# Spreading attention's pieces over all fourteen products of a chunk

## The chip, the cores and the metric

The kernel runs on one core of a Trainium2 chip. The time is device microseconds of one execution, and the median of several executions counts. The core has TensorE (matmul; PE in the profile, its weight loads PEld), VectorE (DVE), ScalarE (ACT), GpSimd (POOL) and SyncE (SP), which here issues transfers between HBM and the on-chip memory SBUF. Matmul results land in PSUM, which the other engines empty. The program gives each engine its own list of instructions; where one needs what another engine or a transfer has yet to make, it waits.

## What is computed

Attention with a decay (retention) over 8 batches, 8 heads, 576 positions and head width 64, and then a two-layer block over the 8 x 576 = 4608 tokens:

```python
scores = scale * np.matmul(q, k.transpose(0, 1, 3, 2))
gamma = 1.0 - 2.0 ** (-5.0 - np.arange(H, dtype=np.float32))
Dmat = np.where(rel >= 0, gamma[:, None, None] ** rel[None, :, :], 0.0)
ret = scores * Dmat[None, :, :, :]
attn_out = np.matmul(ret, v)
# x: (B,H,S,D) -> (B*S, H*D) = 4608 x 512
h = x @ w_in                       # 512 x 2048
sp = np.maximum(h, 0.0) + np.log1p(np.exp(-np.abs(h)))
g = h * erf(sp)
return (g @ w_out).astype(np.float32)   # 2048 x 512
```

## The kernel before

Tokens are handled in 9 chunks of 512. The hidden width is cut in 4 groups, so there are 36 pairs of a first layer and a second layer (`First(g, c)`, `Second`); the first nine pairs are group 0 of each chunk. Each layer of a pair is done in seven products in place of eight (a Strassen-like scheme), a product being four matmuls of 128 x 128 by 128 x 256 in fp32, which the profile shows as eight. So a chunk of one group has fourteen products.

Attention makes the chunks' x while group 0 runs. It goes in 36 pieces of 128 positions, four to a chunk, numbered from 0. A piece has three stages: `transposes` (q and k turned, here by VectorE out of tiles that were loaded as squares), `scores` (32 matmul records, masked by VectorE) and `outputs` (values, state and the x of the piece). The stages stand in one list, and the loop over products takes from it.

The stages (the transposes for pieces from 12 on are VectorE's; the branch with TensorE is cut). The load of q and k of piece i + 2 is issued behind the transposes of piece i; their tiles have two buffers:

```python
    def transposes(i):
        t = live[i] = loaded.pop(i)
        if i < SQUARES:
            weigh_values(i)
        for name in "qk":
            tT = t[name + "T"] = att.tile([P, NP, P], FP32, tag=name + "T", name=name + "T")
            if name + "s" in t:
                for _, _, n, r0 in pieces[i]:
                    a = r0 // SQ * D
                    squares = t[name + "s"][:, :, a : a + n // SQ * D].rearrange("p h (a d) -> p h a d", d=D)
                    order = "p h (a r) -> p h a r" if name == "q" else "p h (r a) -> p h a r"
                    nc.vector.transpose(
                        out=tT[:, :, r0 : r0 + n].rearrange(order, r=SQ), in_=squares[:, :, :, :SQ]
                    )
            else:
                # [... transposes by TensorE for the first pieces ...]
        load(i + 2, "q")

    def scores(i):
        # [... matmuls into ps[0], ps[1] ...]
        mask = tri if len(pieces[i]) == 1 else tri2
        for e in range(2):
            tt(sT[:, e], ps[e], mask.unsqueeze(1).to_broadcast([P, NP, P]), ALU.mult)

    def outputs(i):
        # [... matmuls: values, state update (kv), state times q ...]
        # [... VectorE: sums and state; then x of the piece: ...]
        scaled(1)
        scaled(0)
        load(i + 3, "kv")
        if i + 1 >= SQUARES:
            weigh_values(i + 1)

    stages = [(transposes, 0), (scores, 0)]
    for i in range(len(pieces)):
        stages += [(transposes, i + 1), (outputs, i), (scores, i + 1)]
        if i in (PC + 1, 2 * PC - 1):
            stages[-3:-1] = stages[-2], stages[-3]
    stages = [(of, i) for of, i in stages if i < len(pieces)]
    done = [0]

    def before_chunk(c):

        return stages.index((outputs, c * PC)) if c < n_ch else len(stages)

    def after_chunk(c):

        return stages.index((outputs, (c + 1) * PC - 1)) + 1

    held = [False]

    def attend_next(upto):

        if done[0] < upto and stages[done[0]][0] is outputs:
            held[0] = not held[0]
            if held[0]:
                return
            attend(done[0] + 1)
        attend(min(done[0] + 1, upto))

    def attend(upto):
        while done[0] < min(upto, len(stages)):
            of, i = stages[done[0]]
            of(i)
            done[0] += 1

    PLAIN = 2
```

The products of the first layer (those of the second have the same form). `yield` ends a product; the accumulators `a`, `e` and `g` lie in PSUM, `e` and `g` with one buffer each:

```python
        def first(self):
            self.a = ps_a.tile([P, W], FP32, tag="a", name="a1")
            e = ps_e.tile([P, W], FP32, tag="e", name="e1")

            self.t1 = gpool.tile([P, 2, W], FP32, tag="t1", name="t1")
            self.product(A11, self.a, True)
            nc.scalar.copy(out=self.t1[:, 0], in_=self.a)
            yield
            self.product(A12, e, True)
            tt(self.t1[:, 0], e, self.t1[:, 0], ALU.add)
            yield

        def middle(self):
            self.e = ps_e.tile([P, W], FP32, tag="g", name="g1")
            self.t2 = gpool.tile([P, 2, W], FP32, tag="t2", name="t2")
            self.product(S2, self.a, False)
            nc.scalar.copy(out=self.t1[:, 1], in_=self.a)
            yield
            self.product(S3, self.e, True)
            yield
            self.product(S1, self.a, False)
            nc.scalar.copy(out=self.t2[:, 1], in_=self.a)
            tt(self.t2[:, 1], self.e, self.t2[:, 1], ALU.add)
            yield

        def last(self):
            self.product(S4, self.a, False)
            nc.scalar.copy(out=self.t2[:, 0], in_=self.a)
            yield
            self.product(A22, self.e, False)
            tt(self.t1[:, 1], self.e, self.t1[:, 1], ALU.add)
            self.softplus()
            yield
```

The second layer's products around the accumulator g (`take` empties into the output tile, by ScalarE in group 0; `add` by VectorE):

```python
        def first(self):
            self.a = ps_a.tile([P, 2, OH], FP32, tag="a", name="a2")
            e = ps_e.tile([P, 2, OH], FP32, tag="e", name="e2")
            self.product(B11, self.a, True)
            self.take(0, 0, self.a)
            yield
            self.product(B21, e, True)
            self.add(0, 0, e)
            yield

        def middle(self):
            self.e = ps_e.tile([P, 2, OH], FP32, tag="g", name="g2")
            self.product(T2, self.a, False)
            self.take(1, 0, self.a)
            yield
            self.product(T3, self.e, True)
            yield
            self.product(T1, self.a, False)
            self.take(1, 1, self.a)
            self.add(1, 1, self.e)
            yield

        def last(self):
            self.product(B22, self.a, False)
            self.take(0, 1, self.a)
            self.store(0)
            yield
            self.product(T4, self.e, False)
            self.add(1, 0, self.e)
            self.store(1)
            yield
```

The loop. Behind each product `attend_next` is called once; `most[0]` is the limit up to which attention may go, and `attend(after_chunk(...))` makes sure that a chunk's x is complete before it is read:

```python
    def run(steps, rounds=()):

        for step, _ in enumerate(steps):
            attend_next(most[0])
            round_weights(rounds[step] if step < len(rounds) else 0)

    # [...]
    for b, nxt in zip(blocks[2:], blocks[3:] + [None]):
        n = order.index((b.g, b.c))
        if isinstance(b, First):
            most_g[0] = order[n - 1][0] + 1
            run(b.middle(), (1, 1) if n != 2 else ())
            firsts[n - 1].sums()
            run(seconds[n - 1].first(), (1, 1) if n > 2 else ())
            run(b.last(), (1,) if 2 < n < n_ch else ())
            if n in (2, 3):
                load_weights()
            most[0] = before_chunk(n + 3)
        elif n + 2 < n_s:
            f = firsts[n + 1]
            for step, _ in enumerate(b.middle()):
                attend_next(most[0])
                if step == 0:
                    f.erf()
                elif step == 1 and (n + 2 >= n_ch or done[0] == len(stages)):
                    operands_x(*order[n + 2])
                elif step == 2 and n_ch - 4 < n < n_ch:
                    round_weights()
            if order[n + 2] not in summed:
                attend(after_chunk(n + 2))
                operands_x(*order[n + 2])
            run(nxt.first(), (1,) if n > 1 else ())
            f.multiply()
            seconds[n + 1].begin()
            if n_ch <= n + 3 < n_s:
                load_x(*order[n + 3])
            run(b.last(), (0, 1) if n > 1 else ())
        # [... the last two pairs ...]
```

Of the kernel before, what the change touches and what calls it, by code (L numbers as in the profile page):

```python
# [54 lines left out]
def kernel(  # L55
# [56 lines left out]
    PC = TCH // P  # L112
# [321 lines left out]
    stages = [(transposes, 0), (scores, 0)]  # L434
# [4 lines left out]
    stages = [(of, i) for of, i in stages if i < len(pieces)]  # L439
    done = [0]  # L440
# [6 lines left out]

        return stages.index((outputs, (c + 1) * PC - 1)) + 1

    held = [False]  # L450

    def attend_next(upto):

        if done[0] < upto and stages[done[0]][0] is outputs:
            held[0] = not held[0]
            if held[0]:
                return
            attend(done[0] + 1)
        attend(min(done[0] + 1, upto))

# [5 lines that stand above are left out]
# [287 lines left out]
# [5 lines that stand above are left out]
# [42 lines left out]
    for b, nxt in zip(blocks[2:], blocks[3:] + [None]):  # L800
# [10 lines left out]
# [10 lines that stand above are left out]
# [54 lines left out]
```

## Time and profile before

| What | Value |
|---|---|
| Median of 3 executions | 1025.81 us (1024.72 to 1028.17) |
| The profiled execution | 1028.05 us, span in the profile 1026.2 us |
| Mean granted TensorE clock | 0.997 |
| ScalarE / VectorE busy | 38% / 65% |
| Moved between HBM and SBUF | 165.76 MB, mean 162 GB/s |
| Packets under 512 B | 97376 of 146986 |

In a row of a timeline the first number is the start in us, the second the length; then engine, line of the kernel, operation, output <- inputs, shapes, and how many instructions are merged; in brackets the idle time ahead of it and what ended it. A row of waits has the engine that waited, its tile and line, what it waited for, and then the sum in us, how often, and the longest. L99 is a helper that issues most of VectorE's two-operand instructions, so one goes by the tile names there: t and s are the hidden layer, o the output (also the attention output in PSUM), x the layer's input, g, a and e the accumulators, qT and kT the turned q and k, raw_qs and raw_ks their loaded squares. A row of windows has the stretch, its length, and busy us (and instructions) of PE, PEld, DVE, ACT and POOL, then the granted clock, the share of the transfer engines and GB/s. In the page's part 2 the span is cut in 40 slices of 25.7 us, each digit a busy share in tenths.

### The profile page before, as it was taken

How to read it: one execution, taken by the hardware profiler on the slowest of the kernel's cores; microseconds unless marked ns; L12 is line 12 of the kernel's file. 1: busy time of each engine (PE TensorE's matmuls, PEld its weight loads, DVE VectorE, ACT ScalarE, POOL GpSimd, SP SyncE). 2: the span in 40 equal slices, each digit the busy share in tenths (PEclk: the TensorE clock that was granted, in tenths of full speed). 3: DMA queues.
4: the chain of work that ended last, by engine and by line, in shares of the span. 5: the costliest groups of instructions: out<-in, count | busy, mean ns of one | idle time of the engine just before them, and what ended most of it. 6: DMA issues, size and time to landing. Idle time of an engine off the chain costs nothing.

```text
span 1026.2 us, 15959 instructions
## 1 busy us (share of the span) xinstructions
PE 1013.0 (99%) x6348; PEld 880.4 (86%) x6348; DVE 663.1 (65%) x1062; ACT 390.2 (38%) x481; POOL 120.8 (12%) x122
## 2 busy tenths in 40 slices
PE   9999999989999999999999999999999999999998
PEld 8788888877888888888888888888888888888887
DVE  3769877866976666656666666666567655555555
ACT  2254133233134444433443344444443333333332
POOL 2142122121311110010001001000100000000000
PEclk9999999999999999999999999999999999999999
DMA  9998989979974344544445345444433334444434
GB/s 199 204 246 175 229 205 212 233 168 247 245 176 154 132 144 144 164 164 160 156 146 174 124 144 153 167 152 144 144 124 124 123 128 128 131 134 131 127 87 119
DMA packets 146986, 165.76 MB, mean 162 GB/s; under 512 B 97376, under 2 KB 121568, under 8 KB 138848
## 3 DMA queue, kind: packets, MB, share of 16 engines
q1 hardware_dynamic: 144832, 163.57, 56.6%
q10 hardware_dynamic: 2080, 1.18, 0.5%
q8 instruction: 50, 0.82, 0.3%
q14 instruction: 24, 0.20, 0.1%
HBM read 117.52 MB, written 47.19 MB: 160 GB/s over the span
## 4 chain that ended last, share of the span: by engine, by line
PE 86%; DMA 6%; SPq 3%; DVE 2%; ACT 1%; issue 1%; POOL 1%; ACTq 0%; DVEq 0%; POOLq 0%
PE a L615 22%; PE a L507 22%; PE g L615 11%; PE g L507 11%; PE e L615 6%; PE e L507 5%; PE o L365 2%; PE s L347 2%; DMA raw_v<-in_v_dram 2%; DMA raw_ks<-in_k_dram 2%; SPq L147 2%; DMA raw_k<-in_k_dram 1%; PE o L388 1%; PE o L377 1%; SPq L131 1%; PE f L679 1%
## 5 line engine op out<-in xcount | busy, mean ns | idle before, releaser
L507 PE MATMUL a<-x,wa 128*128 128x256 f32 x1088 | 257.4, 379 | 0.0
L507 PEld LDWEIGHTS a<-x,wa 128*128 128x128 f32 x1088 | 206.4, 190 | 28.4 <-issue 0.2
L615 PE MATMUL a<-wb,s 128*128 128x256 f32 x840 | 199.6, 380 | 0.0
L615 PEld LDWEIGHTS a<-wb,s 128*128 128x128 f32 x840 | 158.7, 190 | 22.8 <-ACT o L629 0.7
L99 DVE TENSOR_TENSOR t<-g,t 128x512 f32<-128x512 f32 x68 | 47.0, 690 | 151.7 <-ACT t L537 114.0
L507 PE MATMUL g<-x,wa 128*128 128x256 f32 x544 | 129.0, 380 | 0.0
L507 PEld LDWEIGHTS g<-x,wa 128*128 128x128 f32 x544 | 102.9, 190 | 14.4
L99 DVE TENSOR_TENSOR o<-a,o 128x512 f32<-128x512 f32 x104 | 71.4, 687 | 46.4 <-PE a L615 46.4
L532 ACT COPY t<-a 128x512 f32<-128x512 f32 x34 | 19.9, 586 | 181.0 <-PE a L507 181.0
L99 DVE TENSOR_TENSOR t<-t,s 128x1024 f32<-128x1024 f32 x72 | 86.9, 1249 | 0.0
L576 ACT ACTIVATE s<-t 128x1024 f32<-128x1024 f32 x72 | 72.1, 1048 | 30.4 <-DVE t L99 30.4
L274 POOL TENSOR_TENSOR wraw<-wraw 128x512 f32<-128x512 f32 x28 | 29.4, 1051 | 444.8 <-DVE wraw L272 190.6
L99 DVE TENSOR_TENSOR x<-x 128x512 f32<-128x512 f32 x115 | 75.9, 694 | 1.2
L543 ACT COPY t<-a 128x512 f32<-128x512 f32 x34 | 19.9, 586 | 146.6 <-PE a L507 146.6
L615 PE MATMUL g<-wb,s 128*128 128x256 f32 x280 | 69.2, 392 | 5.7 <-DVE t L99 5.7
L580 ACT ACTIVATE s<-s 128x1024 f32<-128x1024 f32 x72 | 72.1, 1049 | 0.4
L615 PEld LDWEIGHTS g<-wb,s 128*128 128x128 f32 x280 | 54.3, 195 | 14.4 <-DVE t L99 6.5
L615 PE MATMUL e<-wb,t 128*128 128x256 f32 x280 | 66.5, 380 | 0.0
L615 PE MATMUL a<-wb,t 128*128 128x256 f32 x280 | 66.3, 380 | 0.0
L615 PE MATMUL g<-wb,t 128*128 128x256 f32 x280 | 66.2, 379 | 0.0
L507 PE MATMUL e<-x,wa 128*128 128x256 f32 x272 | 64.5, 380 | 0.0
L99 DVE TENSOR_TENSOR o<-g,o 128x512 f32<-128x512 f32 x70 | 48.0, 686 | 20.7 <-ACT o L629 17.9
(86 smaller groups left out, 1236.6 us busy)
## 6 DMA issues: line engine op xcount, KB each, us to landing
od<-o SPq DMA_DIRECT2D x54, 512.0 KB, 3.3
x<-xd SPq DMA_DIRECT2D x27, 1024.0 KB, 4.8
o<-od SPq DMA_DIRECT2D x27, 1024.0 KB, 4.9
raw_qs<-in_q_dram SPq DMA_DIRECT2D x96, 112.0 KB, 4.5
raw_ks<-in_k_dram SPq DMA_DIRECT2D x84, 112.0 KB, 4.1
xd<-x SPq DMA_DIRECT2D x9, 1024.0 KB, 5.6
raw_v<-in_v_dram SPq DMA_DIRECT2D x64, 128.0 KB, 4.7
wraw<-in_moe_w_in_dram SPq DMA_DIRECT2D x32, 256.0 KB, 5.5
```

The costliest lines, as they stand in the source:

```text
L99: nc.vector.tensor_tensor(out=out, in0=in0, in1=in1, op=op)
L131: nc.sync.dma_start(out=t[part * SQ : (part + 1) * SQ, :, at : at + m - SQ], in_=tokens[:, :, d0 : d0 + m - SQ])
L147: queue.dma_start(out=t[r0 : r0 + n, e::2, :], in_=heads.rearrange("h p d -> p h d"))
L274: engine.tensor_tensor(out=r_f, in0=high_f, in1=r_f, op=ALU.mult)
L347: nc.tensor.matmul(ps[e][:, p, :], lhsT=t["kT"][heads[e], p, :], rhs=t["qT"][heads[e], p, :], start=True, stop=True)
L365: nc.tensor.matmul(o[p % 2][heads[(e + p) % 2], p // 2, :], lhsT=t["v"][:, 2 * p + e, :], rhs=t["sT"][:, e, p, :], start=(p < 2), stop=(no ...
L507: nc.tensor.matmul(acc[:, j * TH : (j + 1) * TH], lhsT=weights["wa", self.g][:, a, d, j * P : (j + 1) * P], rhs=x[self.g, self.c][a][:, d, :],
L532: nc.scalar.copy(out=self.t1[:, 1], in_=self.a)
L543: nc.scalar.copy(out=self.t2[:, 0], in_=self.a)
L576: nc.scalar.activation(self.s[:, j], t, AF.Softplus)
L580: nc.scalar.activation(self.s[:, j], self.s[:, j], AF.Erf)
L615: nc.tensor.matmul(acc[:, tp, :], lhsT=left[:, j * TH + tp * P : j * TH + (tp + 1) * P], rhs=weights["wb", self.g][:, b, j, :], start=(sta ...
```

## The change

Before, each piece waits one product ahead of its outputs: transposes behind one product, nothing behind the next, outputs and the next scores behind the third. Four pieces so take twelve products. From the piece numbered 16 on (the 17th), the odd pieces wait one product more, so that four pieces take 3 + 4 + 3 + 4 = 14 products, as many as a chunk has. It is meant to let attention go at an even pace with the products, where before it ran ahead to its limit and then paused. Nothing else is changed: the same instructions and transfers are issued, some in another order.

```diff
--- before.py
+++ after.py
@@ -447,14 +447,18 @@
 
         return stages.index((outputs, (c + 1) * PC - 1)) + 1
 
-    held = [False]
+    held = [0]
+    EVEN = 4 * PC
 
     def attend_next(upto):
 
-        if done[0] < upto and stages[done[0]][0] is outputs:
-            held[0] = not held[0]
-            if held[0]:
+
+        of, i = stages[done[0]] if done[0] < upto else (None, 0)
+        if of is outputs:
+            held[0] += 1
+            if held[0] <= 1 + (i >= EVEN and i % 2):
                 return
+            held[0] = 0
             attend(done[0] + 1)
         attend(min(done[0] + 1, upto))
```

## The prediction

> **What bounds the kernel now.** I read the page first, then the waits in the part of the span where the change acts, then the timeline around the waits found there, then the same stretches as windows. The page, parts 1 and 2:
>
> ```profile
> PE   1013.0 (99%) x6348; PEld 880.4 (86%) x6348; DVE 663.1 (65%) x1062; ACT 390.2 (38%) x481; POOL 120.8 (12%) x122
> ...
> PE   9999999989999999999999999999999999999998
> PEclk9999999999999999999999999999999999999999
> DMA  9998989979974344544445345444433334444434
> ```
>
> TensorE is busy for 1013.0 of 1026.2 us, so any change that adds and removes no matmul can win little more than the 13.2 us in which it stands, plus matmuls that are stretched. There is one dip, an 8 in the ninth slice (205 to 231 us). The transfers are heavy only in the first twelve slices (to 308 us): that is where attention loads q, k and v. The change touches pieces 17 to 35, whose outputs run from 147 to 317 us in the timeline. The waits of 120 to 325 us:
>
> ```profile
> DVE qT L326 <- DMA raw_qs<-in_q_dram: 7.0, 4, 2.7
> ...
> PE g L615 <- DVE t L99: 5.7, 2, 3.3
> DVE kT L326 <- DMA raw_ks<-in_k_dram: 4.4, 6, 1.2
> ```
>
> TensorE waits twice in there, 5.7 us together, for VectorE to empty the accumulator g; and VectorE's transposes of q and k wait ten times, 11.4 us together, for their loads. The timelines of TensorE and VectorE around the first wait show that these are one thing:
>
> ```profile
> 203.45 1.89 PE L507 MATMUL g<-x,wa 128*128 128x256 f32 x8
> 205.18 1.89 PE L615 MATMUL a<-wb,s 128*128 128x256 f32 x8
> 210.39 3.35 PE L615 MATMUL g<-wb,s 128*128 128x256 f32 x8 [3.32 <-DVE t L99]
> ...
> 217.12 1.99 PE L615 MATMUL a<-wb,s 128*128 128x256 f32 x8
> ```
>
> and of VectorE:
>
> ```profile
> 205.01 0.68 DVE L99 TENSOR_TENSOR o<-e,o 128x512 f32<-128x512 f32 x1
> 207.07 0.71 DVE L326 STREAM_TRANSPOSE qT<-raw_qs 128x512 f32<-128x512 f32 x1 [1.38 <-DMA raw_qs<-in_q_dram]
> 208.40 1.09 DVE L326 STREAM_TRANSPOSE kT<-raw_ks 128x512 f32<-128x512 f32 x1 [0.61 <-DMA raw_ks<-in_k_dram]
> ...
> 209.66 0.67 DVE L99 TENSOR_TENSOR t<-g,t 128x512 f32<-128x512 f32 x1
> ```
>
> VectorE finishes at 205.69, then holds the transposes of piece 25 at its head until q and k have landed, ends them at 209.49, and only then adds g to t (209.66 to 210.33); product T3, which begins g anew, starts at 210.39. Product A22, which filled g, had started at 203.45. The second wait (251.32 us, 2.39 us) has the same form with piece 29. A third piece in that place (33, at 286.92) found its loads landed, and there TensorE doesn't wait.
>
> **What the Trainium skill says.** "PSUM — Partial Sum Buffer", section "Engine vs sequencer instructions": VectorE's queue is a strict FIFO and matmuls start in program order. The lines above agree: an add whose accumulator was full by about 205.3 stood behind a transpose that waited for a load. "TensorE: Matmul & The Clock Gate", Part 1: after idling, TensorE's clock falls to half until it has been busy for some 3.4 us. The trace agrees: the eight matmuls behind the wait span about 3.3 us (210.39 to 213.67, the next block) against 1.73 elsewhere; the windows below give the turns that begin with a wait a mean clock of 0.96. "Perfetto Trace Analysis", section "What 'DMA-bound' means": an issuing engine whose track is solid DMA slices is itself the bound. SyncE's row from 160 to 262 us is nearly that: transfer follows transfer with gaps of 0.1 us.
>
> **What the waits cost.** A product (eight matmuls) takes 1.73 us from start to start (203.45 to 205.18). From T2 to T3 it took 5.21 us the first time (205.18 to 210.39) and 4.28 the second (247.04 to 251.32): 3.48 and 2.55 us lost. Then T3 with one piece's outputs and scores behind it took 6.73 us both times (210.39 to 217.12, 251.32 to 258.05), against 5.00 where there was no wait (290.13 to 295.13): 1.73 us lost twice to the slow clock. Sum 3.48 + 2.55 + 2 x 1.73 = 9.5 us of the profiled execution. I find no other TensorE wait in the part that changes.
>
> **The change part by part.** It adds and removes no engine instruction or transfer; it moves stages among products. I counted the stages through the loop. One turn has products S2 S3 S1 B11 B21 S4 A22 T2 T3 T1 A11 A12 B22 T4. Of a piece, T is its transposes, O its outputs, with the next piece's scores behind them.
>
> Before, once attention has caught up with its limit (from chunk 5): O stands behind T3, A12, S2 and B11, and T behind T1, B22, S3 and B21. S4 and A22 have nothing, since the limit stops the stages there. After, from piece 16: attention keeps the lag of two products it has at piece 16. O stands behind T2, A11, S2 and B11, T behind T3, A12, S3 and B21, and that repeats each turn. Three things follow.
>
> (a) The loads. The load of piece i+2 is asked for when T(i) is emitted and must have landed at T(i+2). Before, that leaves 6, 6, 8 and 8 products; the pieces with 6 (24, 25, 28, 29) have 9.1 of the 11.4 us of load waits. After, it is 7 for all: 7 x 1.73 + 2 x 3.28 = 18.7 us instead of 6 x 1.73 + 2 x 3.28 = 16.9 us for the tight ones (3.28 = 5.00 - 1.73, one piece). Before, chunk 4 and 5 also run at 12 products for four pieces to catch up, and SyncE's row fills there. The windows, by turn, show that:
>
> ```profile
> 138.00:169.64 31.64, 31.64 (x331) 26.98 (x329) 26.78 (x46) 6.75 (x10) 8.72 (x8) 1.00 1.08 239
> 169.64:210.39 40.75, 37.31 (x354) 31.63 (x352) 29.99 (x50) 12.80 (x19) 8.97 (x10) 1.00 0.98 222
> 210.39:251.32 40.93, 38.54 (x352) 32.29 (x353) 28.64 (x51) 12.30 (x17) 7.65 (x8) 0.96 0.83 199
> 251.32:290.13 38.81, 38.81 (x352) 32.91 (x353) 31.06 (x50) 12.94 (x17) 9.15 (x9) 0.96 1.03 240
> ```
>
> The last two numbers are the share of the transfer engines and GB/s. At the fast pace it is 1.08. A turn without loss is 14 x 1.73 + 4 x 3.28 = 37.3 us, the 38.81 of the last row less 1.73 within 0.3, and its transfers fill most of that. The even pace removes the peak, not the sum.
>
> (b) The place of the wait. A T still stands behind B21, ahead of the add that frees g. But now a piece's O and the next scores stand between T2 and T3. T3 then comes 3 x 1.73 + 3.28 = 8.5 us after B21's end, not 5.2. The scores need the same transposes, 3 x 1.73 + 2.2 = 7.4 us after B21's end (2.2 is the piece without its last 1.09 us). In the first wait the transposes ended 209.49 - 201.72 = 7.8 us after it. Late loads of that size would cost 0.4 us, not 3.48, and with 1.8 us more for the load (a) nothing. No idle stretch, so no slow clock.
>
> (c) What gets tighter. A chunk's last O now stands two products before A11, which reads its x: 3.46 us for some 1.2 us of VectorE work (0.42 + 0.74), at a place where VectorE was idle for 5.87 us before. The last piece's outputs end five products (8.6 us) later, but x of the last chunk isn't read before A11 either, and the transfers there have room: from 290 us on, where the loads end, the share is 0.49.
>
> So the gain is 9.5 us of the profiled execution. That one was recorded at 1028.05 us, 2.2 above the median of 1025.81; I take it that part of this is a larger wait than usual, so 7.5 to 9.5 us for the median, minus up to a microsecond that reappears. 1025.8 - 8.3 = **1017.5 us**.
>
> **The rivals.** First, the transfers bind whatever the order: a share of 0.83 to 1.08 speaks for it, and then the scores would wait for kT in place of T3. Against it: in 251.32 to 290.13 all loads came in time at the pace of 37.3 us a turn. It would leave 3 to 9 us of the loss: 1020 to 1026. Second, VectorE gets its work at a worse moment: transposes behind T3 and A12 now stand ahead of the sums of x and of the long multiply (2.4 us), and a late load there delays the add that frees g before S3. Against: between A12 and S3 lie B22, T4, S2 and one piece, 3 x 1.73 + 3.28 = 8.5 us, for 1.8 + 2.4 + 0.7 = 4.9 us of work. One wait with its slow clock would cost 3 to 5 us: 1021 to 1027. Third, nothing is gained since TensorE is 99% busy; but the 9.5 us are counted from starts of products, partly inside busy time.
>
> **Range and chances.** All three leave the time within 2% (20.5 us): the most that can be won is 9.5 us, and to lose 20.5 us some five such waits would have to appear. The range runs from 1014.5 (all of the loss and some luck) to 1024 (one wait left, or the transfers bind in part). Faster by over 2%: 0.01; within 2%: 0.97; slower by over 2%: 0.02.
>
> **What would show it.** Right: no wait of TensorE for t in the middle of the span, no two products in a row over 1.75 us from start to start between 150 and 320 us, no slow-clock block, the ninth slice a 9, load waits of the transposes well under 11.4 us, turns near 37.3 us. Wrong: scores or T3 waiting on kT, qT or t; the load waits as long as before (then (a) is wrong and only (b) may hold); new waits of TensorE after 320 us. What would make the time wrong most easily is a wait that I can't see in this trace because its slack was never used up.

## The result, and the profile after

| | before | changed |
|---|---|---|
| Median, 6 executions each | 1027.48 us | 1020.64 us (1019.22 to 1022.22) |
| Ratio, 95% interval | | 0.9937 (0.9919 to 0.9956) |
| Span of the profiled execution | 1026.2 us | 1019.8 us |
| Wait of TensorE for t ahead of T3, 120 to 325 us | 5.7 us | none |
| Wait of the scores for kT, same stretch | none | 2.4 us |
| Waits of the transposes for their loads, same stretch | 11.4 us | 20.5 us |

The change saves 6.84 us by these medians. The same code, measured again beside two sets of experiments, gave 0.9949 (0.993 to 0.9968) and 0.9963 (0.9948 to 0.9977). The page of the changed kernel, parts 1 and 2:

```profile
PE 1008.4 (99%) x6348; PEld 878.4 (86%) x6348; DVE 662.0 (65%) x1062; ACT 390.0 (38%) x481; POOL 120.0 (12%) x122
...
PE   8999999999999999999999999999999999999998
...
DMA  9997989979976344544444344434333334444434
```

The dip in the ninth slice is gone (the first slice, an 8 now, lies ahead of anything that the change touches). The waits from 120 to 325 us (sum in us, times, longest):

```profile
DVE kT L326 <- DMA raw_ks<-in_k_dram: 11.1, 11, 1.6
...
DVE qT L326 <- DMA raw_qs<-in_q_dram: 9.4, 4, 5.3
...
PE s L347 <- DVE kT L326: 2.4, 1, 2.4
```

So VectorE waits for loads longer than before, and yet TensorE waits less: what counts for TensorE is only whether a transpose has ended when it needs the result. TensorE where T3 had waited before, in the turn of piece 28:

```profile
237.88 1.89 PE L511 MATMUL g<-x,wa 128*128 128x256 f32 x8
...
241.43 1.09 PE L365 MATMUL o<-sT,raw_v 128*64 128x128 f32 x16
...
244.00 1.99 PE L619 MATMUL g<-wb,s 128*128 128x256 f32 x8
```

and VectorE:

```profile
240.34 1.10 DVE L326 STREAM_TRANSPOSE kT<-raw_ks 128x512 f32<-128x512 f32 x1 [0.55 <-DMA raw_ks<-in_k_dram]
...
242.34 0.68 DVE L99 TENSOR_TENSOR t<-g,t 128x512 f32<-128x512 f32 x1
```

The transposes are late again (they end at 241.44, 5.3 us after product B21 ended; 7.8 us in the first wait before) and stand again ahead of the add that frees g (until 243.02). But outputs and scores now fill TensorE from 241.43 to 244.00, and T3 starts on time behind them. What is left is one wait, of the scores for piece 29's kT:

```profile
250.87 0.67 PE L388 MATMUL o<-qT,state 64*64 64x128 f32 x16
253.95 1.16 PE L347 MATMUL s<-qT,kT 64*128 64x128 f32 x16 [2.41 <-DVE kT L326]
255.04 1.99 PE L511 MATMUL e<-x,wa 128*128 128x256 f32 x8
...
258.60 1.89 PE L619 MATMUL g<-wb,t 128*128 128x256 f32 x8
```

and VectorE ahead of it:

```profile
252.72 1.08 DVE L326 STREAM_TRANSPOSE kT<-raw_ks 128x512 f32<-128x512 f32 x1 [1.34 <-DMA raw_ks<-in_k_dram]
```

These transposes stand behind T3, and they end at 253.80, 8.0 us after it (the next product starts at 245.84).

The same three turns, from T3 to T3, as windows (stretch, length, busy us of PE, PEld, DVE, ACT, POOL, clock, share of the transfer engines, GB/s):

```profile
170.29:207.37 37.08, 37.08 (x355) 31.82 (x353) 28.70 (x50) 13.96 (x20) 8.64 (x10) 1.00 1.02 226
207.37:244.00 36.63, 36.63 (x354) 31.37 (x352) 29.59 (x52) 9.22 (x13) 7.73 (x9) 1.00 0.83 203
244.00:283.56 39.56, 37.15 (x355) 31.85 (x353) 29.56 (x51) 14.02 (x20) 8.22 (x9) 1.00 1.03 231
```

They took 40.75, 40.93 and 38.81 us before: 3.67 and 4.30 us saved, 0.75 lost, 7.22 us together, of which the span shows 6.4 (the changed execution entered them 0.65 us later). The third holds the new wait; without it, it would be 37.15 us.

### The profile page after: what moved, and what is told of

Its sections match the earlier page's. It is cut to its first block, busy times and chain, and to the rows that moved or that the text cites. A ratio compares the mean times of both kernels' runs of the same rounds, so it can differ in the third digit from the quotient of the medians.

```text
span 1019.8 us, 15964 instructions
## 1 busy us (share of the span) xinstructions
PE 1008.4 (99%) x6348; PEld 878.4 (86%) x6348; DVE 662.0 (65%) x1062; ACT 390.0 (38%) x481; POOL 120.0 (12%) x122
## 4 chain that ended last, share of the span: by engine, by line
PE 87%; DMA 6%; SPq 4%; DVE 2%; issue 0%; POOL 0%; ACT 0%; DVEq 0%; POOLq 0%; ACTq 0%
PE a L619 23%; PE a L511 22%; PE g L619 11%; PE g L511 11%; PE e L511 6%; PE e L619 6%; PE s L347 2%; PE o L365 2%; SPq L147 2%; SPq L131 2%; DMA raw_qs<-in_q_dram 1%; DMA raw_v<-in_v_dram 1%; DMA raw_ks<-in_k_dram 1%; DMA wraw<-in_moe_w_in_dram 1%; PE o L388 1%; PE o L377 1%
## 5 line engine op out<-in xcount | busy, mean ns | idle before, releaser
L536 ACT COPY t<-a 128x512 f32<-128x512 f32 x34 | 19.9, 585 | 177.7 <-PE a L511 177.7
L547 ACT COPY t<-a 128x512 f32<-128x512 f32 x34 | 19.9, 586 | 152.9 <-PE a L511 152.9
L619 PE MATMUL g<-wb,s 128*128 128x256 f32 x280 | 66.8, 381 | 0.0
L541 ACT COPY t<-a 128x512 f32<-128x512 f32 x34 | 19.9, 585 | 108.7 <-PE a L511 108.7
L619 PEld LDWEIGHTS a<-wb,t 128*128 128x128 f32 x280 | 53.2, 190 | 7.2
```

The lines of the kernel that those rows point to most:

```text
L619: nc.tensor.matmul(acc[:, tp, :], lhsT=left[:, j * TH + tp * P : j * TH + (tp + 1) * P], rhs=weights["wb", self.g][:, b, j, :], start=(sta ...
```

## The experiments

All were timed in five rounds beside the kernel before, whose medians were 1027.93, 1027.13 and 1026.99 us in the three sets. Two reasons for the gain were to be told apart: the **place** (a late load no longer holds up T3) and the **pace** (the loads get equal time and come earlier).

| Run | Median us | Ratio to before, 95% interval | TensorE's waits, 120 to 400 us | Load waits of the transposes, 120 to 325 us |
|---|---|---|---|---|
| changed, again | 1022.86 | 0.9949 (0.993 to 0.9968) | scores 2.5, a 0.5 | 17.2 |
| place_only | 1025.60 | 0.9977 (0.9968 to 0.9986) | scores 5.0 | 14.4 |
| pace_only | 1022.61 | 0.9941 (0.9923 to 0.9959) | T3 2.7 | 7.4 |
| from_21st | 1027.15 | 0.999 (0.9979 to 1.0002) | S3 4.0 | 11.1 |
| after_less | 1017.85 | 0.9914 (0.9901 to 0.9927) | none | 1.1 |
| before_less | 1021.28 | 0.9947 (0.9935 to 0.9959) | T3 2.3, scores 1.2 | 9.1 |
| late_a12 | 1021.83 | 0.9947 (0.9934 to 0.9959) | outputs 0.9, scores 0.6 | 11.5 |
| kv_by_act | 1042.81 | 1.015 (1.0133 to 1.0167) | scores 14.8, others 1.6 | 49.0 |
| before_filled | 1029.77 | 1.0044 (1.0027 to 1.0062) | scores 0.3 (filler in T3's waits) | 10.8 |
| weights_late | 1024.53 | 0.9973 (0.9962 to 0.9985) | T3 3.0, a 1.0, S3 1.0 (all after 318 us) | 0.3 |
| both_late | 1024.35 | 0.9979 (0.9969 to 0.9989) | T3 3.0, a 1.0, S3 1.0 (all after 318 us) | none |
| changed, third time | 1022.85 | 0.9963 (0.9948 to 0.9977) | scores 2.2, a 0.4 | 17.1 |

(All in us; waits of TensorE under 0.3 us are left out.)

### First set: place and pace apart

The changed kernel again:

> The changed kernel once more, beside the three that follow: 1020.6 us within 1.5 on both theories, and a load wait of the transposes near 20 us between 120 and 325 us.

It came 2.2 us above its first median, outside the 1.5, with the same wait of the scores (2.47 us). Where the 2 us go is shown under the third set.

**place_only** is the kernel before with three transposes put behind the add:

```diff
-    def run(steps, rounds=()):
+    def run(steps, rounds=(), keep=()):
         for step, _ in enumerate(steps):
-            attend_next(most[0])
+            if step not in keep or stages[done[0]][0] is not transposes:
+                attend_next(most[0])
...
+            late = 4 <= n <= 6
-            run(seconds[n - 1].first(), (1, 1) if n > 2 else ())
+            run(seconds[n - 1].first(), (1, 1) if n > 2 else (), (1,) if late else ())
-            run(b.last(), (1,) if 2 < n < n_ch else ())
+            run(b.last(), (1,) if 2 < n < n_ch else (), (0,) if late else ())
```

> The kernel before, at its own pace; only the transposes of pieces 25, 29 and 33, which stand behind B21, are put behind A22, so that they stand after the add that frees g. Theory of the place (the gain is that a late load no longer stands ahead of that add, and the pace adds little): TensorE no longer waits for t, no stretched matmuls, 1017 to 1021 us, load waits of the transposes still 8 to 20 us. Theory of the pace (the gain is that the loads get equal time): the loads are as late as before and the wait only moves to the scores behind T3, 3 us or more of it: 1023 to 1028 us.

Neither theory fits. TensorE never waited for t, as the place says, but the scores waited 0.36, 0.45 and 4.19 us for kT. They are not those behind T3, where the theory of the pace looked for the wait: the long one, with stretched matmuls behind it, stands behind S2, with piece 27:

```profile
232.72 2.08 PE L347 MATMUL s<-qT,kT 64*128 64x128 f32 x16 [4.19 <-DVE kT L326]
```

and VectorE ahead of it:

```profile
231.49 1.09 DVE L326 STREAM_TRANSPOSE kT<-raw_ks 128x512 f32<-128x512 f32 x1 [1.76 <-DMA raw_ks<-in_k_dram]
```

The kernel before ran this transpose at nearly the same time (231.34 us), but its TensorE was 4.8 us further behind, because T3 had waited (product T1 started at 217.12, here at 212.36), and its scores didn't wait. So what was won at T3 was lost at the next late load. Of the 5.1 us that the changed kernel saved beside it (1027.93 - 1022.86), 2.3 were left.

**pace_only** keeps the fourteen products, but a chunk's last outputs stand behind T3:

```diff
-            if held[0] <= 1 + (i >= EVEN and i % 2):
+            if held[0] <= (1 if i <= EVEN else (0, 2, 1, 3)[i % PC]):
```

> The changed kernel with its pace of fourteen products, but the outputs of a chunk's last piece stand behind T3 in place of T2, so that T3 again comes 5.2 us after B21 and not 8.5. Theory of the place: T3 waits again for the add behind late transposes, in one to three of the five turns, 1 to 3 us each, some with the slow clock behind it: 1022 to 1027 us. Theory of the pace: as the changed kernel, 1019 to 1022 us.

TensorE in the turn of piece 28:

```profile
236.92 1.89 PE L511 MATMUL g<-x,wa 128*128 128x256 f32 x8
238.65 1.89 PE L619 MATMUL a<-wb,s 128*128 128x256 f32 x8
243.21 3.39 PE L619 MATMUL g<-wb,s 128*128 128x256 f32 x8 [2.67 <-DVE t L99]
```

and VectorE:

```profile
240.49 1.09 DVE L326 STREAM_TRANSPOSE kT<-raw_ks 128x512 f32<-128x512 f32 x1 [0.50 <-DMA raw_ks<-in_k_dram]
...
242.48 0.68 DVE L99 TENSOR_TENSOR t<-g,t 128x512 f32<-128x512 f32 x1
```

This is the clearest look at the place. The transposes end at 241.58, within 0.2 us of the changed kernel's 241.44, and the add within 0.2 us as well. In the changed kernel T3 comes at 244.00 and waits for nothing; here it is due at 240.38 (1.73 behind T2), waits, and runs stretched. (Counted from B21's end the transposes are 1.1 us later here, 6.4 us against 5.3; the changed kernel's add ended 1.0 us before T3 began, so that alone would have cost it some 0.1 us, an estimate.)

Yet the time equals the changed kernel's (0.9941 beside 0.9949; 1022.61 us lies in the range of the place, but so does the changed kernel's 1022.86), since its wait of the scores for piece 29 is absent here. The traces bear out that T3's wait gave that load time to land: SyncE issued piece 29's k squares from 244.69 to 248.60 us here and from 244.57 to 248.73 there, but TensorE came to the scores at 254.85 here and was due at 251.54 there. One wait was exchanged for another. So the place decides where TensorE waits; for the median, T3's cover was not needed. What the fourteen products gain, they gain here with T3 held up.

**from_21st** starts the even pace one chunk later; the transposes that stood behind B21 then stand behind A22:

```diff
-    EVEN = 4 * PC
+    EVEN = 5 * PC
```

> The even pace from the 21st piece on in place of the 17th: pieces 16 to 19 still go at twelve products a chunk, and then all transposes that stood behind B21 stand behind A22, after the add. Theory of the place: no wait for t, scores wait 0 to 3 us, 1017 to 1022 us, no slower than the changed kernel. Theory of the pace: the fast pace of pieces 16 to 19 brings back late loads near 190 to 210 us and with them waits of TensorE: 1022 to 1026 us.

The gain was lost, and by neither of the expected ways: scores hardly waited, and T3 not at all. S3 did, twice. VectorE ahead of the first of them:

```profile
224.91 2.35 DVE L99 TENSOR_TENSOR t<-t,s 128x1024 f32<-128x1024 f32 x2
227.18 0.42 DVE L99 TENSOR_TENSOR sums<-o,state 128x256 f32<-128x256 f32 x1
...
229.37 0.68 DVE L99 TENSOR_TENSOR o<-g,o 128x512 f32<-128x512 f32 x1
```

and TensorE:

```profile
224.24 2.00 PE L619 MATMUL g<-wb,t 128*128 128x256 f32 x8
226.07 1.89 PE L511 MATMUL a<-x,wa 128*128 128x256 f32 x8
230.11 3.13 PE L511 MATMUL g<-x,wa 128*128 128x256 f32 x8 [2.15 <-DVE o L99]
```

S3 begins g anew, as T3 does, only one product behind the one that filled it (T4, then S2). The add that frees it stood behind the sums of x, the multiply and a piece's work; in this first turn two waits for k's squares (1.24 and 1.45 us) ahead of the sums made it later still. Before and in the changed kernel a piece stands between S2 and S3; this order took it away. So g has two such places in a turn. The kernel before covers the one ahead of S3, from_21st neither, pace_only only S3's, and the changed kernel both.

### Second set: why the loads are late

**after_less** and **before_less** leave out one store of 1 MB a turn (x of chunks 4 to 8; the later groups read the x of chunks 0 to 3, so part of the output is of other data):

```diff
-        nc.sync.dma_start(out=x[g, c][:, :n_dc], in_=xd[c])
+        nc.sync.dma_start(out=x[g, c][:, :n_dc], in_=xd[c % PC])
...
-        if g == 0:
+        if g == 0 and c < PC:
             store_x(c)
```

> The changed kernel without the five stores of x of chunks 4 to 8 (1 MB each, one per turn); the later groups read the x of chunks 0 to 3 in their place, so part of the output is of other data. Theory of full transfers (what is left of the load waits comes from transfer engines that are busy all the time): load waits of the transposes fall from 17 to 20 us to under 10, the 2.4 us wait of the scores goes, and the time is 1018 to 1020 us, 2 to 4 under the changed kernel. Theory of a late request (the load is asked for too late whatever else is moved): waits and time as in the changed kernel, 1020 to 1023 us.

> The kernel before, with the same five stores left out. Theory of full transfers: the loads of pieces 25 and 29 come in time, TensorE no longer waits for t, and nearly the whole gain of the change appears without it: 1018 to 1022 us. Theory of a late request: 1026 to 1028 us, with T3 waiting as before.

Both times came out as full transfers say, the first a little better still. In before_less T3 still waited, twice for 1.1 to 1.2 us, and scores once for 1.2 us, but with no stretched matmuls behind. The waits of after_less hold one row of the transposes' loads:

```profile
DVE kT L326 <- DMA raw_ks<-in_k_dram: 1.1, 1, 1.1
```

TensorE waits for nothing in that stretch. Without 1 MB a turn the old order gains 5.9 us of its own, and the changed order 9.3 against the same runs of before. The second is near the 9.5 us that the prediction counted as lost before. With less moved, the change is still worth 3.4 us (1021.28 - 1017.85), as much as TensorE waits in before_less (3.5 us). The share of the transfer engines doesn't tell a late stage from one in time: in the three turns of after_less it is 1.03, 0.84 and 1.12, no lower than in the changed kernel.

**kv_by_act** lets ScalarE issue the row loads of k and v from piece 19 on (EVEN is defined further up for it):

```diff
-                queue = nc.scalar if (name, i) == ("k", 0) else nc.sync
+                queue = nc.scalar if (name, i) == ("k", 0) or i > EVEN + 2 else nc.sync
```

> The changed kernel with the loads of k and v rows of pieces from 19 on issued by ScalarE instead of SyncE. If SyncE's issuing is the bound (its row is full from 160 to 262 us): q and k squares are issued earlier, load waits of the transposes under 8 us, 1017 to 1020 us. If the transfer engines are the bound: load waits stay at 12 to 25 us, and ScalarE's copies come later: 1020 to 1026 us.

Far worse than either: the transposes waited 49.0 us for their loads, 34.3 of it for k's squares and up to 7.5 us at once, and the scores 14.8 us. The median is 1.5% above the kernel before, and some 20 us (2%) above the changed kernel's medians. Taking the row loads off SyncE's queue did not help. That the rows of k and v, asked for three pieces ahead, now compete with squares that are needed sooner is my reading. SyncE's own waits point that way (from 120 to 325 us it stands 41.0 us behind loads of k rows, 0.5 us in the changed kernel), but no run shows it apart.

**late_a12** deals the waits out as 2, 1, 1, 2:

```diff
-            if held[0] <= 1 + (i >= EVEN and i % 2):
+            if held[0] <= 1 + (i >= EVEN and i % PC in (0, 3)):
```

> The changed kernel with the four waits of a chunk dealt out as 2, 1, 1, 2 instead of 1, 2, 1, 2: a chunk's first outputs stand behind A12 in place of A11, the rest as in the changed kernel. The transposes that the scores waited for (2.4 us, piece 29) then have one product, 1.73 us, more. Theory of the place: that wait shrinks to 0 to 1 us, T2 and S2 keep their piece behind them, no wait for t or o: 1018 to 1020.5 us. Against it: the load of the next piece is asked for 1.73 us later and the wait only moves there: as the changed kernel, 1020 to 1023 us.

The wait of the scores fell to 0.6 us, as expected, and the outputs waited 0.9 us for v on GpSimd. The profiled execution ran 1019.73 us, but the median of 1021.83 is above the range, and its interval covers two of the changed kernel's three ratios. It isn't shown to be better.

### Third set: the clock, and moving transfers away

**before_filled** puts idle work into T3's waits of the kernel before:

```diff
                 if step == 0:
+                    if n in (3, 4):
+                        warm = ps_at.tile([P, NP, P], FP32, tag="at", name="warm")
+                        for _ in range(24):
+                            nc.tensor.matmul(warm[:, 0, :], lhsT=ones, rhs=ones, start=True, stop=True)
                     f.erf()
```

> The kernel before with 24 matmuls of ones, whose result nobody reads, behind T2 in the two turns where T3 waited: some 2.6 us of work (an estimate from the 1.09 us of 16 matmul records of 128 columns with the weights changing each time) put into waits of 3.3 and 2.4 us. If the stretched matmuls behind the wait come from the clock that falls when TensorE idles: T3 and the piece behind it take 5.0 us and not 6.73, 2 to 3.5 us saved, less what the filler overruns: 1023.5 to 1026.5 us. If the stretching has another cause (the transfers, VectorE): nothing saved: 1027 to 1030 us.

```profile
249.87 5.52 PE L819 MATMUL warm<-ones 128*128 128x128 f32 x48
255.22 1.89 PE L615 MATMUL g<-wb,s 128*128 128x256 f32 x8
...
260.22 1.99 PE L615 MATMUL a<-wb,s 128*128 128x256 f32 x8
```

My estimate of the filler was half of what it took: 24 matmuls became 48 records, 5.35 us, so the time missed its range and fell in that of the other cause. The lengths of the blocks answer the question all the same: T3 and the piece behind it took 255.22 to 260.22 = 5.00 us, not 6.73, in both turns, and the clock stayed at 1.00. The stretching goes with the idling of TensorE. (In the profile of before, the granted clock of 210.39 to 213.67 us, right behind the first wait, is 0.57.)

**weights_late** and **both_late** round group 1's weights, and so load them, in the turns of chunks 6 to 8; both_late has late_a12's edit as well:

```diff
+    speed = [1]
     def round_weights(n=1):
-        for _ in range(n):
+        for _ in range(n * speed[0]):
...
+            speed[0] = {3: 0, 4: 0, 5: 0, 6: 2, 7: 3, 8: 3}.get(n, 1)
```

> The changed kernel with the rounding of group 1's weights, and so their loads, moved from the turns of chunks 3 to 5 to those of chunks 6 to 8, at two and three steps for one. That moves some 2 MB of transfers out of the part where the q and k squares are late. Theory of full transfers: load waits under 12 us, no wait of the scores, 1017.5 to 1020.5 us. If the rounding crowds VectorE, ScalarE and GpSimd in those turns: new waits of TensorE for t or o after 280 us, 1021 to 1028 us.

> The two edits together: waits dealt 2, 1, 1, 2 and group 1's weights rounded late. If each does what it should, no wait of TensorE above 0.5 us between 120 and 325 us and 1017 to 1020 us; if the late weights crowd the other engines, 1020 to 1027 us.

The waits came as the first half says: load waits fell to 0.3 us, from 17.1 in the changed kernel beside them, and no scores waited. The times did not, since the fear came true as well: T3, S3 and a product on a waited 5.0 us after 318 us, where the rounding stands three steps deep. Both medians lie above that of the changed kernel beside them (1022.85 us). Of the versions here that compute everything, none is shown to beat it.

> The changed kernel, on the same chip as these three: 1020 to 1023 us, one wait of the scores of 2 to 3 us near 250 us.

It did as expected, and its profile explains part of the spread of the changed kernel's times (its 22 executions run from 1017.66 to 1026.25 us). TensorE behind the scores' wait (compare the changed kernel's lines from 253.95 on):

```profile
254.38 2.08 PE L347 MATMUL s<-qT,kT 64*128 64x128 f32 x16 [2.24 <-DVE kT L326]
256.39 3.78 PE L511 MATMUL e<-x,wa 128*128 128x256 f32 x8
259.96 2.34 PE L619 MATMUL a<-wb,s 128*128 128x256 f32 x8
262.13 1.89 PE L619 MATMUL g<-wb,t 128*128 128x256 f32 x8
```

From the scores to the third product behind them it took 7.75 us here (254.38 to 262.13), 6.27 in the second profile and 4.65 in the first (253.95 to 258.60). The wait was the same, 2.2 to 2.5 us; the slow clock behind it cost 3.1, 1.6 and 0 us. The profiled executions took 1024.98, 1023.62 and 1021.55 us.

## Why the prediction was right, and where it wasn't

The median, 1020.64 us, lies in the range, 3.1 us above the point. Of these, 1.7 us are the base: the point was counted from the 1025.81 us of three executions, where six gave 1027.48. The rest is the gain: 8.3 us were forecast, 6.84 measured; the ratios of the repeats, times 1027 us, are gains of 5.2 and 3.8 us.

**What the waits cost** was right: the two turns with a T3 wait lost 3.67 and 4.30 us of their length. The clock's share in it, which the prediction took from two blocks of 6.73 us, was shown by before_filled.

**(a) The loads** was the step that failed. From 7 products for every load the prediction concluded that the loads would come 1.8 us earlier against their need, that load waits would fall "well under 11.4 us", and that with this late transposes would cost nothing. The load waits were 20.5 us, and 17.2 and 17.1 in the repeats. Piece 29's transposes ended 8.0 us after the product that they stand behind, no better than the 7.8 us of piece 25 before. The prediction had reckoned the room for lateness only behind B21, 7.4 us. Behind T3 it is two products and 2.2 us of a piece, 5.7 us by the prediction's own figures; the difference is the wait of 2.41 us. late_a12, which gives one product more there, cut it to 0.6 us. Where the extra time went can be seen in SyncE's row:

```profile
244.57 4.16 SPq L131 DMA_DIRECT2D raw_ks<-in_k_dram  x4
```

Piece 27's transposes freed the buffers at 231.7 us, but SyncE issues one transfer behind another and came to piece 29's k squares only 12.9 us later. Taking 1 MB out of a turn (1.1 us of load waits left) or moving the weights' loads (0.3) brings the loads in time, so what is moved in the turn bounds them; the order counts too, since pace_only (7.4) and late_a12 (11.5) move the same as the changed kernel. The prediction had this as its first rival, and gave it 3 to 9 us. With the slow clock behind it, it cost 2.4 to 5.3 us in the three profiles, the small end.

**(b) The place of the wait** was right for the wait that it looked at: with transposes that end at the same time, T3 is held in pace_only and not in the changed kernel. But the gain doesn't rest on it: pace_only gained as much as the changed kernel beside it, and place_only less than half. What the prediction missed as well is that S3 has the same need. It called the case "VectorE gets its work at a worse moment" and found 8.5 us of room, rightly for this order; from_21st, which has no piece there, paid for it.

**What in the change saves the time**, then, is when TensorE needs the loads. Piece 27's k transposes end at 231.7 us in the changed kernel, 232.5 before and 232.6 in place_only, so this load comes at nearly the same time in all three. But its scores stand behind B11 in the changed kernel and behind S2, three products earlier, in the other two: place_only was due there at 228.5 us and waited 4.2 us; the changed kernel came at 233.2 us and didn't wait. In the same way piece 29's scores stand behind A11 and no longer behind T3. Whether the evenness adds anything to this later need no run shows; the old deal of twelve products, held two or three products back, would be the test.

**The size.** The prediction let "up to a microsecond" reappear. It was 2.41 us in piece 29's scores, and in two of three profiles a slow clock of 1.6 and 3.1 us behind it. In the profiled pair the sum closes: 9.5 - 2.4 = 7.1 us, against 7.22 by the turns. Of its signs, the ninth slice and T3 without a wait appeared, and turns near 37.3 us in two of three; "no slow-clock block" held in the first profile only. Two of its signs of being wrong appeared too: scores that wait for kT, and load waits no shorter than before.

**(c)** held: A11 never waited for x in the changed kernel, and nothing new was lost at attention's later end.

## What to carry to other kernels

Where an in-order engine holds both the emptying of an accumulator and work that waits for a load, look at what stands between the filling and the next use of that accumulator on TensorE: one independent block of 2.6 us there hid a lateness that cost a wait of 2.7 us and a slow clock without it. Check every such reuse before moving work; the block taken from one place was missed at another. But don't count a wait that is hidden as time saved: TensorE then comes sooner to the next late load, and in place_only most of it was lost there. Reckon the room at every place where a load is needed, not only at the one that waits now. And where transfers fill a stage, an even deal of the requests did not make them land in time here; moving less in that stage did.

## What the runs showed of the hardware that was not expected

- Whether TensorE's clock falls behind a wait isn't settled by the wait's length: three profiles of one kernel with waits of 2.41, 2.47 and 2.24 us lost 0, 1.6 and 3.1 us to it. A wait of 1.89 us (from_21st) was followed by a clock of 0.66 over the next 5.0 us. Waits of 1.0 to 1.7 us (before_less, weights_late) showed none.
- Splitting the loads of one stage over two issuing queues made the changed kernel 1.5% slower than the kernel before (1.0133 to 1.0167), where it had been 0.4 to 0.6% faster.
